# Queries loaded in rows of eight tokens and kept in permuted order, with a new order of the whole program

## The chip, the cores and the metric

The kernel runs on one core of one Trainium2 chip. The metric is the device time of one execution in microseconds, as the median of a few runs. A core has five engines with an instruction queue each: TensorE (PE), VectorE (DVE), ScalarE (ACT), GpSimd (POOL) and SyncE (SP). They wait for each other by semaphores. Loads and stores are DMAs, issued here from the queues of POOL and SP and carried out by 16 DMA engines that work for the core.

## The reference, cut to what matters

q, k and v are float32 of shape (8 batches, 8 heads, 576 tokens, 64). w_q and w_k are (512, 64), w_out is (512, 512), the result is (8, 576, 512).

```
scores = q @ k^T / 8
rel    = pos_q - pos_k
scores = where(0 <= rel < 128, scores - slope[head] * |rel|, -1e9)
x      = softmax(scores) @ v                    # heads side by side: (8, 576, 512)
wq, wk = x @ w_q, x @ w_k
mixed  = (wq @ wk^T / 8) @ x                    # over all 576 tokens, no softmax
out    = relu(mixed) @ w_out
```

Each query sees itself and the 127 tokens before it. The second half mixes all tokens of a batch linearly, so the kernel computes wk^T @ x (64 by 512) once per batch and multiplies wq by that.

## The kernel before, in words

All inputs are cast to float16 by the DMAs that load them, except the first ones of batch 0. Per batch b the operations have names, which stand in the order string (line 35) and in this text:

- **Lq, Lk, Lv, Lt** load q, k, v in blocks of 128 tokens, and the last 64 tokens ("tails") of q and k of two batches together (`add_loads`, line 405). A load of one block moves, for 128 tokens and 8 heads, 1024 pieces of 256 bytes. The tile `nat` holds q and k as loaded, in a ring of four batches; `natt` holds the tails, `vt` and `vtl` hold v.
- **Lf, Lh** load q and k of batch 0 in rows of four tokens (`add_first`, line 388), Lf from SP and uncast.
- **TQ** turns q and k by transposes on TensorE, so that the head dimension lies in the partitions (`add_tq`, line 471, and `add_tq0`, line 447, for batch 0). TQb.0 turns q and k of token blocks 0 and 1, TQb.2 those of blocks 2 and 3, 32 transposes each of 64 partitions by 128 columns. **ETQ** copies the result from PSUM (tile `pair`) to `qkT`. TT and ETT do this for the tails.
- **QK** multiplies 128 keys with the 256 queries that can see them, two heads at a time (`add_unit`, line 521). **EXP** is the exponential on ScalarE, from PSUM into `pt`; **MUL** on VectorE multiplies with `bias`, the exponential of the distances with the mask (`add_mul`). `bias` and `biasl` (for the last group) are made once, from a table of distances that POOL's iota writes (line 312).
- **PV** multiplies with v (`add_pv`, line 566); **R** and **X** on VectorE divide by the sums into `x`. PVb.4 does the tails of two batches.
- **XT, EXT** turn x; **WQ, EWQ, EWD, WKT, EWK, G, EG** make wq, wk and wk^T @ x; **MX, RM** mix and apply the relu; **OUT, EO** multiply with w_out and copy to `osb`; **DO** stores 128 tokens (line 819). Stores of batches 0 to 5 go from POOL, and each of them waits until all loads have been issued (line 876); `osb` has 26 buffers (HELD), so that early results are held until then. Stores of batches 6 and 7 go from SP.

The order of everything is written out by hand in the string ORDER: each word is an operation, the engine it runs on, for TensorE the PSUM banks, and after a + how many filling matmuls (of zeros, into the same bank) stand ahead of it. `Graph.ordered` (line 145) emits them in that order, so each engine's queue is the string's words for that engine. An engine takes its queue strictly in order. Copies out of PSUM may stand on ScalarE or VectorE, as the string says.

The waits are set from the operations' dependencies; TQ waits for its loads, a load into the ring waits for the TQ that read the old contents four batches before.

Of the kernel before, what the change touches and what calls it, by code (L numbers as in the profile page):

```python
# [9 lines left out]
F16 = mybir.dt.float16  # L10
# [30 lines left out]
ETQ0.1.1.1@DVE TT0@PE:1 EXP0.0.1@ACT Lv0.3@POOL QK0.1.1@PE:0 EXP0.2.0@ACT Lk1.0@POOL MUL0.0@DVE
QK0.2.1@PE:3 EXP0.1.1@ACT Lv0.2@POOL ETT0@DVE ETT1@DVE QK0.3.1@PE:2+1 Lq1.1@POOL EXP0.2.1@ACT MUL0.1@DVE
Lq1.0@POOL TQ1.2@PE:0+1 EXP0.3.1@ACT MUL0.2@DVE PV0.0@PE:1 Lk1.1@POOL ETQ1.2@ACT QK0.3.0@PE:3 R0.0@DVE
biasl1@DVE Lv0.4@POOL EXP0.3.0@ACT QK1.3.1@PE:2+1 X0.0@DVE QK1.3.0@PE:0 Lv1.3@POOL EXP1.3.1@ACT
MUL0.3@DVE PV0.1@PE:3 Lv1.2@POOL EXP1.3.0@ACT R0.1@DVE Lw1@POOL PV0.2@PE:2+2/10 X0.1@DVE QK1.2.0@PE:1
R0.2@DVE PV0.3@PE:0 X0.2@DVE EXP1.2.0@ACT Lq2.1@POOL XT0.0@PE:3 R0.3@DVE MUL1.3@DVE QK1.2.1@PE:2
Lq2.0@POOL EXP1.2.1@ACT TQ1.0@PE:1 X0.3@DVE Lv1.1@POOL EXT0.0@ACT ETQ1.0@DVE XT0.1@PE:2 Lk2.0@POOL
EXT0.1@ACT PV0.4@PE:0 Lk2.1@POOL QK1.1.0@PE:1 R0.4@DVE QK1.0.0@PE:3 X0.4@DVE EXP1.1.0@ACT QK1.1.1@PE:2
pads@POOL MUL1.2@DVE WQ0.0@PE:00 Lv1.0@POOL EXP1.1.1@ACT QK1.0.1@PE:1 XT0.2@PE:01 Lk2.3@POOL EXT0.2@DVE
EXP1.0.0@ACT MUL1.1@DVE WQ0.1@PE:01 Lk2.2@POOL PV1.3@PE:2 EXP1.0.1@ACT PV1.2@PE:3 R1.3@DVE Lq2.2@POOL  # L50
X1.3@DVE EWQ0.0@ACT XT1.2@PE:10 EWQ0.1@ACT R1.2@DVE Lq2.3@POOL X1.2@DVE WKT0@PE:11+1 TQ2.0@PE:2 EWK0@DVE
Lwo2@POOL EXT1.2@DVE ETQ2.0@ACT G0@PE:11 MUL1.0@DVE Lwo1@POOL XT1.1@PE:0 EG0@ACT Lwo3@POOL QK2.0.0@PE:3
EXT1.1@ACT PV1.0@PE:2 Lwo0@POOL PV1.1@PE:1 EXP2.0.0@ACT R1.0@DVE Lt2.0@POOL X1.0@DVE QK2.0.1@PE:0
EWD0@ACT R1.1@DVE WQ1.1@PE:30 Lt2.1@POOL EXP2.0.1@ACT X1.1@DVE MX0.0@PE:2 EWQ1.1@DVE Lv2.1@POOL
XT1.0@PE:1 RM0.0@DVE TQ2.2@PE:0 EXT1.0@ACT Lq3.2@POOL MX0.1@PE:3 ETQ2.2@ACT WQ1.0@PE:10 RM0.1@DVE
Lk3.2@POOL EWQ1.0@ACT QK2.1.1@PE:2 EWD1@ACT QK2.2.0@PE:0 Lk3.3@POOL MUL2.0@DVE WKT1@PE:11 EXP2.1.1@ACT
QK2.2.1@PE:3 OUT0.3@PE:10 Lq3.3@POOL EWK1@DVE EXP2.2.1@ACT G1@PE:11 Lq3.0@POOL EO0.3@DVE EXP2.2.0@ACT
QK2.1.0@PE:2 EG1@DVE TT2@PE:3 Lv2.0@POOL OUT0.2@PE:10 ETT3@DVE EXP2.1.0@ACT ETT2@DVE Lk3.0@POOL
QK2.3.0@PE:0 EO0.2@DVE MX1.0@PE:3 EXP2.3.0@ACT MX1.4@PE:2 Lv2.2@POOL OUT0.0@PE:11 RM1.0@DVE Lk3.1@POOL
RM1.4@ACT MX1.1@PE:0 EO0.0@ACT QK2.3.1@PE:2 MUL2.2@DVE OUT0.1@PE:10 Lq3.1@POOL RM1.1@ACT MUL2.1@DVE  # L60
# [105 lines left out]
def kernel(  # L166
# [145 lines left out]
    def mk_iota(o):  # L312
        nc.gpsimd.iota(wint, pattern=[[1, 256]], base=0, channel_multiplier=-1)
# [603 lines left out]
```

## Time and profile before

| | |
|---|---|
| median of 3 runs | 134.95 us (134.85 to 134.96) |
| the profiled execution | 135.62 us, its span 133.6 us |
| around the span | 2.0 us |
| granted TensorE clock, mean | 0.974 |
| DMA packets | 111431, of which 105840 under 512 B |
| moved by DMA | 25.12 MB, mean 188 GB/s |
| HBM read and written | 29.62 MB and 9.44 MB |

The profile gives the busy time of each engine, then groups of instructions by line, with their count, their total and the mean duration of one in ns, and the idle time before them with what ended it. A row of the instructions in order of time has start, time covered, engine, line, tiles and shapes. A stretch of several equal instructions is one row, and its time is that of the whole stretch, in which neighbours overlap. "issue" as a reason means that the profile shows nothing that the engine waited for. A tile name such as nat stands for all its buffers. The DMA share in a table by stage is a mean over the 16 engines of the time of the packets under way, which can be more than one at once.

### The profile page before, as it was taken

How to read it: one execution, taken by the hardware profiler on the slowest of the kernel's cores; microseconds unless marked ns; L12 is line 12 of the kernel's file. 1: busy time of each engine (PE TensorE's matmuls, PEld its weight loads, DVE VectorE, ACT ScalarE, POOL GpSimd, SP SyncE). 2: the span in 40 equal slices, each digit the busy share in tenths (PEclk: the TensorE clock that was granted, in tenths of full speed). 3: DMA queues.
4: the chain of work that ended last, by engine and by line, in shares of the span. 5: the costliest groups of instructions: out<-in, count | busy, mean ns of one | idle time of the engine just before them, and what ended most of it. 6: DMA issues, size and time to landing. Idle time of an engine off the chain costs nothing.

```text
span 133.6 us, 5403 instructions
## 1 busy us (share of the span) xinstructions
PE 120.6 (90%) x2356; PEld 78.1 (58%) x2356; DVE 110.2 (82%) x186; ACT 113.1 (85%) x166; POOL 109.7 (82%) x148
## 2 busy tenths in 40 slices
PE   6884999689889999999999999999999899999950
PEld 2551567556646566757766576667666556775520
DVE  6528888899898999998997999999999899968240
ACT  6778886697999999999999999999999899765630
POOL 7985999999999999999999999999966158871000
PEclk9999658999999999999999999999999999999999
DMA  3999999999999999999999999999999729998973
GB/s 107 259 167 157 157 151 152 140 148 142 183 155 160 153 155 152 154 156 157 159 149 152 156 154 156 158 151 154 155 202 395 302 93 285 355 326 304 355 264 94
DMA packets 111431, 25.12 MB, mean 188 GB/s; under 512 B 105840, under 2 KB 108656, under 8 KB 111408
## 3 DMA queue, kind: packets, MB, share of 16 engines
q0 software_dynamic: 108896, 21.37, 179.4%
q1 hardware_dynamic: 2512, 3.41, 7.4%
q8 instruction: 18, 0.29, 0.9%
q14 instruction: 5, 0.04, 0.1%
HBM read 29.62 MB, written 9.44 MB: 292 GB/s over the span
## 4 chain that ended last, share of the span: by engine, by line
PE 46%; ACT 23%; DMA 11%; POOL 7%; DVE 6%; issue 4%; ACTq 0%; POOLq 0%; DVEq 0%
PE pair L229 40%; ACT pt L551 13%; DMA natt<-in_q_dram 7%; PE pair L232 5%; DMA vt<-in_v_dram 5%; POOL nat L380 4%; ACT qkT L242 3%; DVE x L615 2%; ACT osb L236 2%; DVE pt L561 2%; ACT rm L755 1%; ACT wqd L242 1%; POOL vt L380 1%; DVE inv L612 1%; ACT gs L236 1%
## 5 line engine op out<-in xcount | busy, mean ns | idle before, releaser
L551 ACT ACTIVATE pt<-pair 128x1024 f16<-128x1024 f32 x64 | 63.2, 1039 | 4.0 <-PE pair L229 2.6
L229 PE MATMUL pair<-wout_sb,rm 128*128 128x512 f16 (+1 forms) x132 | 31.9, 373 | 0.2 <-ACT wkn L242 0.2
L380 POOL DMA_DIRECT2D vt<-in_v_dram x32 | 30.2, 1044 | 2.1 <-DMA natt<-in_q_dram 1.6
L561 DVE TENSOR_TENSOR pt<-pt,bias 128x2048 f16<-128x2048 f16 x24 | 29.0, 1216 | 1.4 <-ACT pt L551 1.4
L380 POOL DMA_DIRECT2D nat<-in_q_dram x29 | 27.8, 988 | 0.3 <-issue 0.2
L380 POOL DMA_DIRECT2D nat<-in_k_dram x29 | 27.7, 993 | 0.0
L229 PE MATMUL pair<-qkT 64*128 64x256 f16 (+2 forms) x320 | 23.6, 258 | 0.8 <-ACT qkT L242 0.3
L229 PEld LDWEIGHTS <-pt 128*128 128x128 f16 (+1 forms) x576 | 19.3, 102 | 7.1 <-issue 3.2
L615 DVE TENSOR_TENSOR x<-pair,inv 128x512 f16<-128x512 f32 x32 | 22.1, 690 | 0.9
L229 PE MATMUL pair<-vt,pt 128*128 128x65 f16 (+1 forms) x512 | 22.0, 196 | 0.6 <-DMA vt<-in_v_dram 0.5
L822 POOL DMA_DIRECT2D out_dram<-osb x24 | 13.4, 576 | 8.1 <-DVE osb L238 4.3
L229 PEld LDWEIGHTS <-rm 128*128 128x128 f16 x132 | 11.4, 97 | 11.2 <-issue 1.2
L236 ACT COPY osb<-pair 128x512 f32<-128x512 f32 (+1 forms) x24 | 13.7, 582 | 3.9 <-PE pair L229 3.2
L229 PEld LDWEIGHTS <-qkT 64*128 64x128 f16 x320 | 11.8, 97 | 7.6 <-issue 3.1
L242 ACT COPY qkT<-pair 128x1024 f32<-128x1024 f32 (+1 forms) x13 | 12.7, 980 | 1.3 <-PE pair L232 1.1
L757 DVE TENSOR_SCALAR rm<-pair 128x1024 f16<-128x1024 f32 (+1 forms) x10 | 11.0, 1113 | 1.6 <-PE pair L229 1.5
L238 DVE COPY osb<-pair 128x512 f32<-128x512 f32 x13 | 8.9, 687 | 4.0 <-PE pair L229 3.9
L232 PE MATMUL pair<-identh,nat 64*128 64x64 f16 (+1 forms) x512 | 10.6, 194 | 0.7 <-ACT pt L551 0.3
L229 PE MATMUL pair<-xT,wqk_sb 128*128 128x256 f16 (+1 forms) x64 | 10.1, 286 | 0.9 <-DVE xT L244 0.4
L232 PEld LDWEIGHTS <-nat 64*128 64x128 f16 (+1 forms) x512 | 9.3, 98 | 2.8 <-issue 1.3
L612 DVE RECIPROCAL inv<-pair 128x8 f32<-128x8 f32 x36 | 7.3, 203 | 4.1 <-PE pair L229 3.2
L561 DVE TENSOR_TENSOR pt<-pt,biasl 128x2048 f16<-128x2048 f16 x8 | 9.7, 1207 | 0.4 <-ACT pt L551 0.4
(73 smaller groups left out, 165.1 us busy)
## 6 DMA issues: line engine op xcount, KB each, us to landing
out_dram<-osb POOLq DMA_DIRECT2D x24, 256.0 KB, 5.1
vt<-in_v_dram POOLq DMA_DIRECT2D x32, 128.0 KB, 5.9
nat<-in_q_dram POOLq DMA_DIRECT2D x28, 128.0 KB, 5.5
nat<-in_k_dram POOLq DMA_DIRECT2D x28, 128.0 KB, 5.5
out_dram<-osb SPq DMA_DIRECT2D x7, 256.0 KB, 2.9
out_dram<-osb POOLq DMA_DIRECT2D x6, 128.0 KB, 4.9
nat<-in_q_dram SPq DMA_DIRECT2D x1, 512.0 KB, 3.9
nat<-in_k_dram SPq DMA_DIRECT2D x1, 512.0 KB, 4.9
```

The source lines that it names most:

```text
L229: hold(nc.tensor.matmul(*a, **k))
L232: hold(nc.tensor.transpose(*a))
L236: hold(nc.scalar.copy(out_ap, in_ap))
L238: hold(nc.vector.tensor_copy(out=out_ap, in_=in_ap))
L242: hold(nc.scalar.copy(out_ap.bitcast(FP32), in_ap.bitcast(FP32)))
L380: op = add(kind, b, part, (eng,), deps, lambda o: q.dma_start(out=dst, in_=src), size=size)
L551: nc.scalar.activation(out=pt[:, u, 0:1024], in_=two(s.bank).rearrange("p e c -> p (e c)"), func=AF.Exp, scale=SCALE)
L561: nc.vector.tensor_tensor(out=pt[:, :, 0:1024], in0=pt[:, :, 0:1024], in1=bt, op=ALU.mult)
L612: nc.vector.reciprocal(out=box["inv"], in_=px(64))
L615: nc.vector.tensor_tensor(out=x.rearrange("p (g h d) -> p g h d", g=2, h=4), in0=px(slice(0, 64)), in1=box["inv"].unsqueeze(3).broadcast_t ...
L757: hold(nc.vector.tensor_scalar(out=out_ap, in0=in_ap, scalar1=0.0, scalar2=WSCALE, op0=ALU.max, op1=ALU.mult))
L822: q.dma_start(out=out[b, P * st:P * st + P, c], in_=osb)
```

## The change

**Loads of q, batches 1 to 7.** The four loads of a batch become two. Lqb.0 takes heads 0 to 3, Lqb.1 heads 4 to 7. Each has 64 partitions with 4 heads of 8 successive tokens: 256 pieces of 2 KB of float32, into half of the partitions of `nat`. Partition p of a half holds tokens 8p to 8p + 7. k and v are loaded as before.

**Turning.** TQb.0 now turns all of q of a batch, TQb.1 all of k. q takes 64 transposes of 64 by 64 (head half e, head group u), two of which share the rows and two the columns of TensorE's array; k takes 32 of 64 by 128. The first QK of a batch thus needs all of q and k, where it needed blocks 0 and 1.

**The order of queries.** Turning leaves the queries sorted by token mod 8; ETQ writes them so that each block of 128 tokens has 8 groups of 16, group t holding the tokens with token mod 8 = t. Everything behind the scores carries that order (rows of pt, x, wq, mixed, osb). The table of distances is written in the same order (iota), and `biasl`, whose last quarter belongs to the tails in their plain order, is made by three copies in place of two. For batch 0, whose q is loaded in rows of four tokens, each copy of q becomes four copies of a quarter. The stores put the rows back: a store goes to 8 groups of 16 rows, each row 2 KB.

**The order string** is new as a whole. Operations move between ScalarE and VectorE, and the filling matmuls go from 17 to 31, now with the last of them before XT0.1.

```
-iota@POOL Lf0.0@SP ident@POOL Lf1.0@SP dist@DVE mask@DVE Lh0.1@POOL empty@DVE bias0@ACT Lh1.1@POOL
+iota@POOL Lf1.0@SP ident@POOL Lf0.0@SP dist@DVE empty@DVE pads@POOL ones@DVE Lh1.1@POOL mask@DVE
...
-        nc.gpsimd.iota(wint, pattern=[[1, 256]], base=0, channel_multiplier=-1)
+        nc.gpsimd.iota(wint, pattern=[[128, 2], [1, 8], [8, 16]], base=0, channel_multiplier=-1)
...
-            for c, n in ((0, 192), (192, 64)):
-                cpw(o.eng, dst[:, :, c:c + n], src[:, :, 0:n])
+            cpw(o.eng, dst[:, :, 0:P], src[:, :, 0:P])
+            for c, a in ((P, P), (192, 0)):
+                cp(o.eng, dst[:, :, c:c + 64].rearrange("p x (q t) -> p x q t", t=8),
+                   src[:, :, a:a + P].rearrange("p x (t q) -> p x q t", t=8)[:, :, 0:8])
...
+                    elif n < 2:
+                        loads[b, j, n] = load(
+                            "Lq", b, n, ("c", 256, 2048), old,
+                            nat_s[b % NNAT][j][64 * n:64 * n + 64].rearrange("p n h d -> p (n h d)").rearrange(
+                                "p (h c) -> p h c", h=4),
+                            t[b, 4 * n:4 * n + 4, 0:512, :].rearrange("h (p t) d -> p h (t d)", t=8))
...
+                    for c in range(2):
+                        for r in range(2):
+                            cp(o.eng, dst[:, c].rearrange("p (n r t q) -> p r n t q", n=2, r=2, t=4)[:, r],
+                               src[:, c].rearrange("p t (n q r) -> p r n t q", n=2, r=2)[:, r])
...
+                for c in range(2):
+                    for t in range(8):
+                        for e in range(2):
+                            for u in range(2):
+                                r = slice(64 * u, 64 * u + 64)
+                                tp(bank[64 * e:64 * e + 64, u, c, t], rows[r, 2 * c + e, t], identh[r, r])
...
+                cpw(o.eng, dst.rearrange("p c (n t q) -> p c t n q", n=4, t=8),
+                    bank.rearrange("p u (c t n q) -> p (u c) t n q", c=2, t=8, n=4))
...
-            need = [evt[b, g], evt[b, g + 1]] if g < 3 else [evt[b, 3], ett[b]]
+            need = [evt[b, 0], evt[b, 1]] + ([] if g < 3 else [ett[b]])
...
-                q.dma_start(out=out[b, P * st:P * st + P, c], in_=osb)
+                q.dma_start(out=out[b, P * st:P * st + P, c].rearrange("(p t) c -> t p c", t=8), in_=osb)
```

POOL's queue near the program's start, before (nat10 and nat11 are q and k of batch 1, nat20 and nat21 those of batch 2; the shape is partitions x pieces x elements):

```order
L380 DMA nat10_75<-in_q_dram 128x8x64
L380 DMA vt_85<-in_v_dram 128x8x64 x3
L380 DMA nat11_76<-in_k_dram 128x8x64
L380 DMA vt_85<-in_v_dram 128x8x64
L380 DMA nat10_75<-in_q_dram 128x8x64 x2
L380 DMA nat11_76<-in_k_dram 128x8x64
L380 DMA vtl_86<-in_v_dram 64x16x64
L380 DMA vt_85<-in_v_dram 128x8x64 x2
L380 DMA wqk_sb_71<-in_moe_w_k_dram 128x4x64
L380 DMA nat20_77<-in_q_dram 128x8x64 x2
L380 DMA vt_85<-in_v_dram 128x8x64
L380 DMA nat21_78<-in_k_dram 128x8x64 x2
```

and now, the same stretch:

```order
L381 DMA nat10_75<-in_q_dram 64x4x512
L381 DMA nat11_76<-in_k_dram 128x8x64 x2
L381 DMA vt_85<-in_v_dram 128x8x64 x4
L381 DMA nat21_78<-in_k_dram 128x8x64
L381 DMA vt_85<-in_v_dram 128x8x64
L381 DMA nat20_77<-in_q_dram 64x4x512
L381 DMA vtl_86<-in_v_dram 64x16x64
L381 DMA nat20_77<-in_q_dram 64x4x512
L381 DMA nat21_78<-in_k_dram 128x8x64 x3
L381 DMA wqk_sb_71<-in_moe_w_q_dram 128x4x64
```

The last load of batch 2's q or k stands a few rows behind vtl now (the end of the x3 row); before, four of its eight loads came later than the rows shown.

ScalarE's queue in batches 0 and 1, before (L551 is EXP, L242 and L236 are copies out of PSUM: qkT is ETQ, xT is EXT, wqk is EWQ):

```order
L242 COPY qkT_84<-pair_117 128x2x8x2x32
L551 ACTIVATE pt_90<-pair_120 128x1024
L551 ACTIVATE pt_91<-pair_119 128x1024
L551 ACTIVATE pt_91<-pair_117 128x1024
L551 ACTIVATE pt_88<-pair_118 128x1024
L551 ACTIVATE pt_88<-pair_119 128x1024
L242 COPY xT_103<-pair_120 128x2x4x2x32
L242 COPY xT_103<-pair_119 128x2x4x2x32
L551 ACTIVATE pt_87<-pair_118 128x1024
L551 ACTIVATE pt_87<-pair_119 128x1024
L551 ACTIVATE pt_92<-pair_120 128x1024
L551 ACTIVATE pt_92<-pair_118 128x1024
```

and now, from the copy of batch 1's q on (L580 is EXP, L241 a copy):

```order
L241 COPY qkT_84<-pair_117 128x4x8x4x8
L580 ACTIVATE pt_90<-pair_119 128x1024
L580 ACTIVATE pt_91<-pair_117 128x1024
L580 ACTIVATE pt_92<-pair_118 128x1024
L580 ACTIVATE pt_91<-pair_119 128x1024
L580 ACTIVATE pt_92<-pair_120 128x1024
L580 ACTIVATE pt_88<-pair_119 128x1024
L580 ACTIVATE pt_87<-pair_120 128x1024
L241 COPY xT_103<-pair_117 128x2x4x2x32
L580 ACTIVATE pt_88<-pair_120 128x1024
L580 ACTIVATE pt_87<-pair_118 128x1024
```

Seven exponentials stand in a row where there were five and then two copies of turned x; on TensorE, PV0.4 stood ahead of four of batch 1's score units (QK1.1.0, QK1.0.0, QK1.1.1, QK1.0.1) and stands ahead of one now (QK1.2.0).

SP's queue at the end, before (L822 is a store of 128 tokens, L825 one of 64):

```order
L822 DMA out_dram<-osb_2964 128x512
L822 DMA out_dram<-osb_2982 128x512
L822 DMA out_dram<-osb_2989 128x512
L825 DMA out_dram<-osb_2992 64x512 x2
```

and now:

```order
L851 DMA out_dram<-osb_3204 8x16x256
L851 DMA out_dram<-osb_3212 8x16x512
L854 DMA out_dram<-osb_3220 64x512 x2
L851 DMA out_dram<-osb_3228 8x16x512
L851 DMA out_dram<-osb_3231 8x16x512
```

The two stores of 64 tokens stood last and stand third from the end now; a store's DRAM side has 8 groups of 16 rows in place of 128 rows.

More of the change, by code (lines that the diff above doesn't have):

```diff
@@ L41 @@
[L41 to L60, printed above, removed]
@@ L118 @@
+DO7.4@SP OUT7.0@PE:01 EO6.0@DVE DO6.0@SP EO7.0@ACT DO7.0@SP
 """
@@ L495, in add_tt @@
+        old = [qkd.get((b - 2, g, u)) for g in range(4) for u in range(2)]
+        evt[b, j] = add("ETQ", b, j, EV, [t, *old], ev, frees=[t], size=2)
     def add_tt(pr):
```

201 lines of the change are left out of this document (113 added, 88 removed).

## The prediction

> **What bounds the kernel now.** I read the page first, then the busy time by stage, then the instructions in order of time around the holes, then the chain.
>
> ```profile
> span 133.6 us, 5403 instructions
> PE 120.6 (90%) x2356; PEld 78.1 (58%) x2356; DVE 110.2 (82%) x186; ACT 113.1 (85%) x166; POOL 109.7 (82%) x148
> PE 46%; ACT 23%; DMA 11%; POOL 7%; DVE 6%; issue 4%; ACTq 0%; POOLq 0%; DVEq 0%
> ```
>
> The third line is the chain that ended last: mostly TensorE, then ScalarE, with loads and their issuing on GpSimd (DMA and POOL, 18%) before that. By stage, columns PE, PEld, DVE, ACT, POOL busy, then clock, DMA share and GB/s:
>
> ```profile
> 10.00:20.00 10.00, 7.87 (x119) 4.56 (x119) 8.24 (x13) 8.61 (x10) 8.41 (x10) 0.71 2.41 155
> 20.00:30.00 10.00, 8.28 (x193) 6.19 (x190) 8.62 (x14) 7.44 (x10) 10.00 (x16) 0.95 2.36 147
> 30.00:40.00 10.00, 9.08 (x203) 6.05 (x201) 9.13 (x16) 8.74 (x15) 9.84 (x14) 1.00 2.01 160
> 60.00:70.00 10.00, 9.91 (x219) 6.99 (x219) 9.27 (x18) 9.67 (x15) 10.00 (x13) 1.00 2.42 155
> 90.00:100.00 10.00, 9.74 (x224) 7.01 (x222) 9.61 (x17) 9.90 (x13) 8.95 (x13) 1.00 2.40 167
> ```
>
> Three regimes. From 40 us on TensorE, ScalarE, VectorE and GpSimd are all over 90% busy: nothing there gets faster unless work goes away. From 10 to 40 us ScalarE idles 1.39 + 2.56 + 1.26 = 5.2 us while GpSimd does nothing but issue loads. And at the end TensorE runs alone. So the change, which takes work from GpSimd alone, can only pay in the second regime. The three largest ScalarE holes there:
>
> ```profile
> 22.18 1.02 ACT L551 ACTIVATE pt<-pair 128x1024 f16<-128x1024 f32 x1 [1.09 <-issue]
> 25.71 0.19 PE L229 MATMUL pair<-vt,pt 128*64 128x65 f16 x1 [0.51 <-DMA vt<-in_v_dram]
> 26.75 3.77 ACT L551 ACTIVATE pt<-pair 128x1024 f16<-128x1024 f32 x4 [1.06 <-PE pair L229]
> 31.98 1.01 ACT L242 COPY qkT<-pair 128x1024 f32<-128x1024 f32 x1 [0.87 <-PE pair L232]
> ```
>
> 1.09 + 1.06 + 0.87 = 3.0 us. The second has its cause in the row above it: PV0.4 waits for a v load on TensorE, with the scores of batch 1 queued behind it. The third waits for TQ2.0, the turning of batch 2's q and k.
>
> **The change part by part.** *Loads.* Prices of a POOL load, start to start, from rows with 1024, 512 and 128 pieces:
>
> ```profile
> 1.63 0.90 POOL L380 DMA_DIRECT2D nat<-in_q_dram  x1
> 2.53 0.78 POOL L380 DMA_DIRECT2D nat<-in_k_dram  x1
> 27.33 1.81 POOL L380 DMA_DIRECT2D nat<-in_k_dram  x2
> 29.07 1.82 POOL L380 DMA_DIRECT2D nat<-in_q_dram  x2
> 30.80 2.24 POOL L380 DMA_DIRECT2D wout_sb<-in_moe_w_out_dram  x4
> 32.91 0.96 POOL L380 DMA_DIRECT2D natt<-in_q_dram  x1
> 94.44 2.16 POOL L380 DMA_DIRECT2D vt<-in_v_dram  x2
> ```
>
> 1024 pieces of 256 B: (29.07 - 27.33)/2 = 0.87 us. 128 rows of 2 KB: (32.91 - 30.80)/4 = 0.53. 512 rows of 1 KB: 0.75 to 0.90. A new q load has 256 rows of 2 KB; I take 0.62, nearer the 2 KB rows. 28 x 0.87 - 14 x 0.62 = 24.4 - 8.7 = 15.7 us less on GpSimd (bounds 11.8 at 0.90, 16.9 at 0.53). None of it is on the end's path after 40 us. What it moves: batch 2's last q or k load is issued at 29.07 + 0.87 = 29.9 now. In the new queue nothing but 22 loads and three memsets stands before Lk2.3; added up at these prices from about 2 us, that is 21 us, and an estimated 23.5 with waits for earlier loads. The last load of all, at 95.3 us now, would go near 81. So TQ2.0 and TQ2.1 can run some 6 us sooner. PV0.4 also moves: it stood ahead of four score units of batch 1, in the new order ahead of one, so that its wait no longer blocks ScalarE.
>
> I count the three holes as gone: -3.0. Against it stands a late start. The q copies of batch 0 now go in four pieces each:
>
> ```profile
> L236 ACT CAST wkn<-pair 128x128 f16<-128x128 f32 x1 | 0.3, 266 | 0.0
> 7.44 1.07 ACT L236 CAST qkT<-pair 128x512 f16<-128x512 f32 x2 [1.67 <-PE pair L229]
> 8.51 1.94 ACT L551 ACTIVATE pt<-pair 128x1024 f16<-128x1024 f32 x2
> ```
>
> Four times 0.266 is 1.06, in place of one of some 0.6: the first exponential comes at about 8.95, not 8.51, +0.45. Start: -2.55 (bounds: -4.75 if all 5.2 us go; -0.65 if one hole goes).
>
> *ScalarE's load.* Beyond its place, the order gives work to ScalarE. Counted up to the last exponential it gets 4 output copies, 4 of wkn, 2 tails, 3 of wq, 2 small relus, 1 of xT more; 3 of G, 3 large relus, 1 of qkT fewer; and three added pieces. The main prices:
>
> ```profile
> L236 ACT COPY osb<-pair 128x512 f32<-128x512 f32 x22 | 13.0, 601 | 3.4 <-PE pair L229 2.8 <-DMA out_dram<-osb 0.6
> L755 ACT ACTIVATE rm<-pair 128x1024 f16<-128x1024 f32 x6 | 6.3, 1043 | 0.7 <-PE pair L229 0.7
> L236 ACT CAST gs<-pair 128x256 f16<-128x256 f32 x5 | 1.9, 373 | 0.1
> L242 ACT COPY wkn<-pair 128x160 f32<-128x160 f32 x2 | 0.6, 292 | 0.2
> L242 ACT COPY qkT<-pair 128x256 f32<-128x256 f32 x1 | 0.4, 372 | 0.0
> L236 ACT CAST wqk<-pair 128x320 f16<-128x320 f32 x4 | 1.8, 454 | 0.2 <-PE pair L229 0.2
> ```
>
> 4 x 0.60 + 4 x 0.29 + 2 x 0.37 + 3 x 0.42 (between gs and the 320 row) + 2 x 0.39 + 0.58 - 3 x 0.37 - 3 x 1.04 - 1.03 + 0.47 = +2.1 us by durations. But instructions that follow each other overlap: four exponentials took 3.77 us in the row at 26.75, so each after the first costs 0.91, 0.13 less than its 1.04. With 12 instructions more that takes 1.5 off: +0.6, which I take; the ends are 0.6 and 2.1. VectorE gets about as much less, which helps only where it was late. The added q copy in runs of 16 is priced as before, since it moves the same 128x1024 words.
>
> *TensorE.* Per batch q is turned by 64 transposes of 64 by 64 in place of 32 on 64 by 128. Both kinds are in the trace:
>
> ```profile
> 8.88 0.45 PE L232 MATMUL pair<-identh,nat 64*64 64x64 f16 x32
> 23.25 0.64 PE L232 MATMUL pair<-identh,nat 64*128 64x64 f16 x32
> L232 PE MATMUL pair<-identh,nat 64*64 64x64 f16 x64 | 0.9, 195 | 0.2 <-DMA nat<-in_k_dram 0.2
> L232 PEld LDWEIGHTS <-nat 64*64 64x64 f16 x64 | 0.7, 108 | 0.6 <-DMA nat<-in_k_dram 0.3 <-issue 0.2
> ```
>
> One takes 195 ns, but 32 take 0.45 us, so they follow at (0.45 - 0.195)/31 = 8 ns; the half-array ones at (0.64 - 0.19)/31 = 14.5. 64 x 8 - 32 x 14.5 = 0.05 to 0.07 us per batch, seven times: +0.5. At 14.5 each it would be 7 x 0.46 = +3.3, the upper bound. [...] The 14 extra fill matmuls stand before 25 us, where TensorE waits anyway.
>
> *The tail.* Behind the last scores TensorE has one OUT more (OUT5.2), without WQ6.0 and XT7.2:
>
> ```profile
> 110.44 1.89 PE L229 MATMUL pair<-wout_sb,rm 128*128 128x512 f16 x8
> 109.99 0.61 PE L229 MATMUL pair<-xT,wqk_sb 128*128 128x256 f16 x4
> 109.97 1.95 ACT L551 ACTIVATE pt<-pair 128x1024 f16<-128x1024 f32 x2
> 128.96 0.58 ACT L236 COPY osb<-pair 128x512 f32<-128x512 f32 x1 [1.60 <-PE pair L229]
> 122.48 6.72 SPq L822 DMA_DIRECT2D out_dram<-osb  x9
> 129.56 1.16 SPq L825 DMA_DIRECT2D out_dram<-osb  x2
> out_dram<-osb SPq DMA_DIRECT2D x7, 256.0 KB, 2.9
> out_dram<-osb SPq DMA_DIRECT2D x4, 128.0 KB, 2.6
> ```
>
> An OUT paces at about 0.9 us ((1.89 - 0.3)/2, and its start), a WQ at 0.45: +0.3 with XT7.2. The last store was two of 128 KB, issued in 1.16; now one of 256 KB, issued in 0.36 (as the nine in 6.72, less waits): -0.8, and its landing 2.9 for 2.6: +0.3. Together -0.5. That the last rows are strewn 16 KB apart in DRAM I price at nothing here; they are still whole 2 KB rows.
>
> Sum: -2.55 + 0.6 + 0.5 + 0.3 - 0.5 = -1.65. The profiled execution took 135.62 (span 133.6), 0.67 above the median of 134.95; it would become 133.97, and the median 133.3.
>
> **The rivals.** *Slower: ScalarE is the limit and the holes move.* The mechanism: in the middle the chain passes to ScalarE for 23% of the span, and each microsecond given to it there is paid. The price is the full 2.1, the late first exponential 0.45, one hole recovered -1.1, tail +0.3 - 0.5: +1.25, 136.2. It decides once less than 2.5 us of the 5.2 idle on ScalarE before 40 us go. For it: ScalarE is 97 to 99% busy later. Against it: VectorE is relieved, and no hole of the start lay in ScalarE itself.
>
> *The stores go at half rate.* A store's DRAM side is now 8 groups of 16 rows, where it was 128 rows. If only half of the DMA engines serve such a store, the transfer part of its landing doubles: 2.9 - 2.6 = 0.3 per 128 KB, so 0.6 more for the last, and nine stores issued in 6.72 us would need about 8 x 1.2 = 9.6 us of transfer, a queue of up to 2.9 us; I count a third of it, since the last four stores come 0.9 apart: +0.9, and +1.5 in all, 134.8. Nothing in this trace shows it: every load and store there has an outermost count of 64 or 128. [...]
>
> *The loads do not come sooner.* If the bytes set the pace and not the pieces, a q load of 512 KB read takes as long as two old ones (2 x 0.87) and the issue saving is taken back by transfers. Then PV0.4 alone gains by its place: of the three holes half go, +1.5 on the sum, 134.8. For it: the DMA engines show a share over 2 in every stage; against it, weight loads of 2 KB rows go at 0.53, and the share fell to 2.01 behind them.
>
> **How the numbers follow.** A measurement of this kernel can tell about 0.2% (0.27 us). Forecast 133.3: 0.45. Slower rival 136.2: 0.25. Half-rate stores 134.8: 0.18. Loads no sooner 134.8: 0.12. The middle two lie at -0.1%, so each is split: of their 0.30, 0.11 faster, 0.11 same, 0.08 slower. Faster: 0.44 + 0.11 = 0.55, same 0.01 + 0.11 = 0.12, slower 0.25 + 0.08 = 0.33. Range: down to all 5.2 us of the start recovered, 133.3 - 2.2 = 131.1; up to the slower rival with 0.3 for drains between transposes, 136.5.
>
> **What would show it.** Right: POOL q loads of some 0.62 us start to start; the last load issued near 81 us; ScalarE busy over 9 of 10 us from 20 to 30 us; blocks of 64 small transposes in 0.7 us. The slower rival shows as the last exponential ending later than 109.97 + 1.95 = 111.9 us, where it ends now. Half-rate stores show as SP stores of 256 KB landing 3.5 us or more after issue. Wrong altogether: idle ScalarE after 40 us, behind TensorE, which would mean that the new order has holes of its own.

## The result, and the profile after

The changed kernel takes 155.3 us (154.95 and 155.61), the kernel before beside it 134.9 (134.2 to 134.96): a ratio of 1.149 (1.142 to 1.155), 20 us slower where 1.65 us faster was forecast. (Times in this document are medians of the executions within 1.5% of the fastest of their kernel, one for `e1_plain` and two for the changed kernel; the profiled executions of `e1_plain`, `h2_double_plain`, `f3_before_twice` and `h3_half_paced` lie outside, so stops and waits are read from them but no total times.) The profiled execution took 155.61 us, its span 153.8.

The page of the changed kernel: span, busy time by engine, two queues and the chain that ended last.

```profile
span 153.8 us, 5894 instructions
PE 125.3 (81%) x2594; PEld 79.8 (52%) x2594; DVE 110.1 (72%) x189; ACT 116.0 (75%) x177; POOL 96.0 (62%) x134
...
q0 software_dynamic: 85120, 21.38, 137.7%
q1 hardware_dynamic: 2440, 3.41, 7.0%
q8 instruction: 20, 0.33, 0.8%
...
PE 57%; ACT 12%; issue 11%; DVE 10%; POOL 0%; POOLq 0%; ACTq 0%; DVEq 0%
```

GpSimd's busy time fell by 13.7 us, near the 15.7 forecast, and it has gone from the chain (7% before). In its place stands "issue" with 11% (4% before): time in which an engine waited for nothing that the profile shows. By stage, as in the prediction's table:

```profile
10.00:20.00 10.00, 8.01 (x229) 4.66 (x223) 6.25 (x13) 9.28 (x11) 9.12 (x11) 1.00 2.13 168
20.00:30.00 10.00, 8.68 (x247) 5.93 (x238) 9.49 (x16) 7.85 (x10) 7.96 (x10) 1.00 2.09 168
30.00:40.00 10.00, 7.61 (x140) 5.50 (x139) 6.38 (x13) 7.14 (x11) 9.19 (x13) 0.83 1.80 178
60.00:70.00 10.00, 9.90 (x222) 6.95 (x219) 9.10 (x18) 9.65 (x16) 9.03 (x12) 1.00 2.18 165
90.00:100.00 10.00, 8.07 (x166) 5.85 (x160) 6.37 (x13) 6.50 (x11) 7.18 (x13) 0.83 1.45 231
```

In some stages TensorE, VectorE and ScalarE are each idle for 1.9 to 3.6 us (30 to 40, 90 to 100). The granted clock is 0.83 in these two: it is 0.5 for 3.4 us from 33.4 and from 94.9 us, about 1 us behind the end of the two longest stops below, and matmuls are slower there as well (one of 128x320 took 473 ns from 33.4 to 36.8 us, 297 from 36.9 to 50). TensorE's waits for loads come to 0.4 us in all. Its part in the list of waits (total us, times, longest) and what it did there:

```profile
PE pair L231 <- issue: 8.9, 6, 2.4
...
PEld L231 <- issue: 13.4, 19, 2.5
```

```profile
28.86 0.70 PE L231 MATMUL pair<-identh,nat 64*64 64x64 f16 x64 [0.34 <-ACT xT L241]
...
29.83 0.22 PE L231 MATMUL pair<-identh,nat 64*128 64x64 f16 x2
32.45 0.59 PE L231 MATMUL pair<-identh,nat 64*128 64x64 f16 x29 [2.39 <-issue]
```

The block of 64 small transposes takes 0.70 us, as priced. Then TensorE stops for 2.4 us in the middle of k's transposes, whose loads have landed. Before, the same view has 4.7 us in 15 waits, the longest 0.7, and the page fewer pieces on queue q8:

```profile
PEld L232 <- issue: 4.7, 15, 0.7
...
q8 instruction: 18, 0.29, 0.9%
```

Counted from 0 in the records of the trace, weight loads, matmuls and a few waits together (5188 and 13), the stops of over 1 us in 64-partition transposes come at TensorE's instructions 705, 1217, 2241, 3009, 3777 and 4289: all of them 193 + 256 k. Queue q8 brings instructions, 20 pieces of 16 KB here and 18 before, against 5201 and 4721 TensorE instructions: one piece for about 256. So I call a **gap** the time between the starts of instructions 192 + 256 k and 193 + 256 k where it is over 0.4 us, and a fetch's **delay** the time from the start of instruction 193 + 256 k to the start of the next piece on q8 (mean over blocks begun from 15 to 95 us). Before: no gap, delay 2.07 us. After: gaps of 10.0 us in all, delay 3.25 us.

The end moved as well. Last output copy and SP's stores, of the changed kernel:

```profile
139.62 0.59 ACT L235 COPY osb<-pair 128x512 f32<-128x512 f32 x1 [1.14 <-PE pair L228]
132.49 10.12 SPq L851 DMA_DIRECT2D out_dram<-osb  x7
142.71 3.13 SPq L854 DMA_DIRECT2D out_dram<-osb  x2
145.93 1.36 SPq L851 DMA_DIRECT2D out_dram<-osb  x2
out_dram<-osb SPq DMA_DIRECT2D x4, 128.0 KB, 6.7
```

From the end of the last copy to the end of the span it takes 153.8 - 140.2 = 13.6 us, where it took 133.6 - 129.5 = 4.1. (Of the four stores of 128 KB one has a recorded landing.) And behind 140 us, with nothing but stores left, the DMA engines are half busy (last two columns: share and GB/s):

```profile
135.00:140.00 5.00, 4.58 (x32) 2.27 (x24) 1.81 (x3) 2.98 (x7) 0.00 (x0) 1.00 0.68 188
140.00:145.00 5.00, 0.00 (x0) 0.00 (x0) 0.00 (x0) 0.20 (x1) 0.00 (x0) 0.76 0.52 174
145.00:150.00 5.00, 0.00 (x0) 0.00 (x0) 0.00 (x0) 0.00 (x0) 0.00 (x0) 0.50 0.57 155
```

So two things are to be explained: some 10 us of TensorE stops, and some 10 us of stores.

### The profile page after: what moved, and what is told of

It is laid out like the page before. It is cut to its first block, busy times and chain, and to the rows that moved or that the text cites. A ratio compares the mean times of both kernels' runs of the same rounds, so it can differ in the third digit from the quotient of the medians.

```text
span 153.8 us, 5894 instructions
## 1 busy us (share of the span) xinstructions
PE 125.3 (81%) x2594; PEld 79.8 (52%) x2594; DVE 110.1 (72%) x189; ACT 116.0 (75%) x177; POOL 96.0 (62%) x134
## 3 DMA queue, kind: packets, MB, share of 16 engines
q0 software_dynamic: 85120, 21.38, 137.7%
## 4 chain that ended last, share of the span: by engine, by line
PE 57%; ACT 12%; issue 11%; DVE 10%; POOL 0%; POOLq 0%; ACTq 0%; DVEq 0%
PE pair L228 49%; PE pair L231 8%; ACT pt L580 6%; DVE pt L590 4%; ACT bias L345 2%; ACT osb L235 2%; DVE x L644 2%; ACT qkT L235 1%; DVE qkT L243 1%; ACT biasl L235 1%; DVE inv L641 1%; DVE vtl L330 1%; DVE xtl L644 0%; DVE nat L316 0%; ACT xT L241 0%
## 5 line engine op out<-in xcount | busy, mean ns | idle before, releaser
L580 ACT ACTIVATE pt<-pair 128x1024 f16<-128x1024 f32 x64 | 63.3, 1033 | 6.8 <-PE pair L228 6.4
L381 POOL DMA_DIRECT2D vt<-in_v_dram x32 | 28.5, 896 | 2.8 <-DMA nat<-in_q_dram 1.4
L381 POOL DMA_DIRECT2D nat<-in_k_dram x29 | 25.8, 898 | 5.6 <-DMA vt<-in_v_dram 4.0
L851 POOL DMA_DIRECT2D out_dram<-osb x24 | 14.4, 603 | 23.7 <-ACT rmt L784 17.3
L235 ACT COPY osb<-pair 128x512 f32<-128x512 f32 (+1 forms) x29 | 16.7, 582 | 4.7 <-PE pair L228 4.6
L231 PE MATMUL pair<-identh,nat 64*64 64x64 f16 (+1 forms) x736 | 11.1, 193 | 7.3 <-issue 7.0
L231 PEld LDWEIGHTS <-nat 64*64 64x64 f16 (+1 forms) x736 | 9.2, 104 | 9.8 <-issue 8.7
L241 ACT COPY qkT<-pair 128x1024 f32<-128x1024 f32 (+1 forms) x14 | 12.4, 886 | 1.6 <-PE pair L231 1.6
L786 DVE TENSOR_SCALAR rm<-pair 128x1024 f16<-128x1024 f32 (+1 forms) x11 | 12.3, 1124 | 1.0 <-PE pair L228 0.7
L228 PE MATMUL pair<-xT,wqk_sb 128*128 128x256 f16 (+1 forms) x64 | 11.5, 314 | 0.1
L228 PE MATMUL pair<-fill 128*128 128x512 f16 x31 | 9.5, 437 | 1.4 <-DVE fill L361 1.2
L381 POOL DMA_DIRECT2D nat<-in_q_dram x15 | 9.9, 662 | 1.1 <-DMA nat<-in_q_dram 0.5
L590 DVE TENSOR_TENSOR pt<-pt,biasl 128x2048 f16<-128x2048 f16 x8 | 9.7, 1217 | 0.7 <-ACT pt L580 0.7
```

The costliest lines, as they stand in the source:

```text
L228: hold(nc.tensor.matmul(*a, **k))
L231: hold(nc.tensor.transpose(*a))
L235: hold(nc.scalar.copy(out_ap, in_ap))
L241: hold(nc.scalar.copy(out_ap.bitcast(FP32), in_ap.bitcast(FP32)))
L381: op = add(kind, b, part, (eng,), deps, lambda o: q.dma_start(out=dst, in_=src), size=size)
L580: nc.scalar.activation(out=pt[:, u, 0:1024], in_=two(s.bank).rearrange("p e c -> p (e c)"), func=AF.Exp, scale=SCALE)
```

## The experiments

Times with the 95% interval of the ratio to the kernel before. Gaps and delays are those of the one profiled execution of each.

| run | us | ratio | TensorE instructions | delay | gaps, us |
|---|---|---|---|---|---|
| before | 134.9 | 1 | 4721 | 2.07 | 0 |
| after | 155.3 | 1.142 to 1.155 | 5201 | 3.25 | 10.0 |
| `e1_plain` | 144.3 | one run | 5201 | 3.48 | 12.4 |
| `e2_sixteen` | 145.1 | 1.064 to 1.088 | 5201 | 3.28 | 9.5 |
| `e3_before_groups` | 147.7 | 1.083 to 1.107 | 4721 | 1.97 | 0.9 |
| `e4_before_rows` | 137.0 | 1.003 to 1.026 | 4721 | 2.79 | 4.4 |
| `f3_before_twice` | 137.0 | 1.007 to 1.022 | 5169 | 2.18 | 2.3 |
| `h1_half_plain` | 136.7 | 1.008 to 1.021 | 4753 | 3.07 | 1.9 |
| `h2_double_plain` | 144.7 | 1.066 to 1.084 | 5201 | 3.30 | 9.3 |
| `g1_mix` | 149.6 | 1.100 to 1.121 | 5201 | 2.87 | 6.5 |
| `e5_paced` | 137.7 | 1.013 to 1.026 | 4721 | 1.68 | 1.2 |
| `d1_after_paced` | 140.8 | 1.038 to 1.052 | 5201 | 1.88 | 2.9 |
| `e6_rows_first` | 135.7 | two runs | 4721 | 1.86 | 2.0 |
| `e7_both_rows` | 138.3 | 1.021 to 1.041 | 4721 | 2.73 | 3.2 |
| `h3_half_paced` | 139.4 | 1.032 to 1.041 | 4753 | 1.96 | 0 |
| `d2_paced_all` | 142.2 | 1.053 to 1.060 | 5201 | 1.70 | 0 |

### The stores: `e1_plain`, `e2_sixteen`, `e3_before_groups`

The first two alter only the stores of the changed kernel (`e1_plain` above, `e2_sixteen` below), the third puts its store into the kernel before.

```
-q.dma_start(out=out[b, P * st:P * st + P, c].rearrange("(p t) c -> t p c", t=8), in_=osb)
+q.dma_start(out=out[b, P * st:P * st + P, c], in_=osb)
...
+q.dma_start(out=out[b, P * st:P * st + P, c].rearrange("(p t) c -> t p c", t=16), in_=osb)
```

> The changed kernel, but each store of 128 tokens goes to 128 rows of DRAM in the order in which they lie in osb, so the output rows of a block stay in the order of the queries (token mod 8). All else is as changed. Half-rate theory (only 8 of the 16 DMA engines serve a store with 8 groups): the 9.5 us at the end go, last compute to end of span falls from 13.6 to about 4 us, the run takes 146 to 147 us, SP's 128 KB stores land within 3 us of their issue; last compute stays near 140 us, since the TensorE stalls stay. Rival, the stores queue only because they were held back on GpSimd by the order of the stores: the end stays about 13 us after the last compute.

> The changed kernel, but a store has 16 groups of 8 rows on its DRAM side where it had 8 groups of 16; the rows of a block are strewn over DRAM as in the changed kernel, but land in other places than they should. Theory that the number of groups sets how many DMA engines serve a store: as with plain rows, 146 to 147 us and some 4 us from last compute to the end. Rival, rows strewn 16 KB apart in DRAM cost the time (pages, address jumps): as the changed kernel, some 155.6 us and 13 us.

> The kernel before, with one edit: each store of 128 tokens goes to 8 groups of 16 rows, as in the changed kernel, so the rows land in other places than they should. Half-rate theory: last compute to the end of the span grows from 4.1 us to 11 to 14 us and the time to 142 to 145 us; last compute stays near 129.5. Rival, the end of the changed kernel is late because of its order and not because of its groups: within 1 us of 135.

Measured: 144.3, 145.1 and 147.7 us; the theory's ranges were missed by 1 to 3 us, below for the first two and above for the third. From the end of the last copy to the end of the span it takes 3.8 us with plain rows (as in `h1_half_plain` below) and 4.6 with 16 groups, against 13.6 with 8, though with 16 groups the rows of a group lie twice as far apart in DRAM (32 KB in place of 16). So strewn rows are not the main cause, the number of groups is. In the kernel before, 8 groups alone cost 12.8 us. Its SP stores, its last copy, and its end by stage:

```profile
122.10 15.07 SPq L822 DMA_DIRECT2D out_dram<-osb  x9
137.27 2.90 SPq L825 DMA_DIRECT2D out_dram<-osb  x2
128.58 0.59 ACT L236 COPY osb<-pair 128x512 f32<-128x512 f32 x1 [1.60 <-PE pair L229]
130.00:135.00 5.00, 0.00 (x0) 0.00 (x0) 0.00 (x0) 0.00 (x0) 0.00 (x0) 0.75 0.62 179
135.00:140.00 5.00, 0.00 (x0) 0.00 (x0) 0.00 (x0) 0.00 (x0) 0.00 (x0) 0.50 0.53 190
```

The nine stores take 15.07 us to issue, where they took 6.72, though SP waited for their data no longer than before (2.5 us, 3.3 before): it is held by something that no view names. The last copy stays (129.2, before 129.5), and 16.6 us of storing follow it in place of 4.1. The same stage of `e2_sixteen`:

```profile
135.00:140.00 5.00, 3.05 (x15) 1.18 (x12) 1.38 (x2) 1.95 (x5) 0.00 (x0) 1.00 0.93 289
```

A share of 0.93 at 289 GB/s against 0.53 at 190. The half-rate theory has 8 of the 16 DMA engines serve a store with 8 groups. The trace does not tell the engines apart, so that itself is not shown, but these shares, near a half with 8 groups and near the whole with 16, agree with it. The rivals written down for the three runs fall. So does one that the changed kernel's page suggests: GpSimd stands still for 17.3 us ahead of one store there, and the DMA share from 110 to 120 us is 0.07. In `e2_sixteen` the same wait is 16.4 us long, and its stores still end 4.6 us after the last copy.

### The stops: `e4_before_rows`, `h1_half_plain`, `h2_double_plain`, `f3_before_twice`

If TensorE stops because its next 256 instructions have not come, two things make it: instructions used up faster, and fetches that come later. These four runs separate the two. `e4_before_rows` gives the kernel before the large q loads (each turning of a batch then waits for both of them):

```
+elif n < 2:
+    loads[b, j, n] = load("Lq", b, n, ("c", 256, 2048), old,
+        nat_s[b % NNAT][j][64 * n:64 * n + 64].rearrange("p n h d -> p (n h d)").rearrange(
+            "p (h c) -> p h c", h=4),
+        t[b, 4 * n:4 * n + 4, 0:512, :].rearrange("h (p t) d -> p h (t d)", t=8))
```

`h1_half_plain` and `h2_double_plain` (with its inner loop) take the changed kernel with plain stores, and other transposes of q; `f3_before_twice` does each q transpose of the kernel before twice:

```
-for e in range(2):
-    for u in range(2):
-        r = slice(64 * u, 64 * u + 64)
-        tp(bank[64 * e:64 * e + 64, u, c, t], rows[r, 2 * c + e, t], identh[r, r])
+for u in range(2):
+    r = slice(64 * u, 64 * u + 64)
+    for _ in range(2):
+        tp(bank[:, u, c, t], flat[r, 8 * c + t], identh[r, r])
...
+for _ in range(2 - j):
     flip(halves(o.bank, 8, len(ns))[:, h, NHP * j + c, i, :], src.rearrange("p a b -> p (a b)"), h)
```

> The kernel before, with q of batches 1 to 7 loaded by two DMAs of 256 pieces of 2 KB in place of four of 1024 pieces of 256 B; everything else, the order too, as before (the values of q land in other places than the transposes take them from, so the scores are wrong). My forecast's theory of the loads: GpSimd is some 15 us less busy, the loads come sooner, and one or two of the three holes of ScalarE before 40 us shrink: 132 to 134.5 us. Rival, the larger loads delay TensorE's instruction fetches and so make the stalls by themselves: 138 us or more, with gaps at every 256th instruction. Third, loads no sooner: 134.9 within 0.5.

> The changed kernel with stores to plain rows and with the q of batches 1 to 7 turned by 32 transposes of 64 by 128 a batch (the arrangement of q in qkT is then not the one that the scores need) in place of 64 of 64 by 64: 448 TensorE instructions less. Measured against e2_sixteen (145.1 us, with 9.5 us of gaps at TensorE instructions 193 + 256 k). Fetch theory (TensorE stalls where the next 256 instructions have not been fetched, because the 64-transposes use them up faster than the fetches come): the gaps fall to about what e4_before_rows has, 3 to 5 us, and the time to 137 to 140 us. Rival, small transposes cost by changing the array's tiling: the gaps go wholly, 135.5 us or less. Rival, the gaps come from the loads and the order alone: they stay, 144 to 145 us.

> As h1_half_plain, but each of the 32 transposes of q is done twice: the number of TensorE instructions is that of the changed kernel again (5201), with no transpose of 64 by 64 for q. Fetch theory: gaps at instructions 193 + 256 k with a sum of 8 to 11 us, 143.5 to 147 us. Rival, the tiling by 64 by 64 makes the gaps: as h1_half_plain, within 1.5 us of it.

> The kernel before, with each transpose of q of batches 1 to 7 done twice: 448 TensorE instructions more, loads, order and stores as before. Fetch theory: gaps of over 0.4 us appear at instructions 193 + 256 k, fewer than with the 2 KB loads, whose fetches start later (mean 2.1 us after the block before, 2.8 to 3.3 there): a sum of 2 to 6 us, and the time up by as much and by 7 x 0.5 us of transposing, 138 to 144 us. Rival, gaps come with the 2 KB loads alone: no gap over 0.4 us, 135 to 139 us.

In `e4_before_rows` TensorE runs the program of the kernel before, instruction by instruction, and stops nevertheless: 1.58, 0.45, 1.21, 0.71 and 0.46 us, each at 193 + 256 k. With the loads alone changed the delay went from 2.07 to 2.79 us, and the kernel is 2.1 us slower, not 0.4 to 2.9 us faster: my theory of the loads missed, its rival (138 or more) was a little high.

448 transposing instructions more cost 2.1 us with the old loads (`f3_before_twice`, gaps 2.3 us, the time a little below its forecast) but 8.4 us with the new (`e2_sixteen` less `h1_half_plain`, gaps 7.6 us more) or 8.0 (`h2_double_plain` less `h1_half_plain`). These pairs differ in the order of the program too; the next section has a pair that does not. And the tiling is not what makes the stops: `h2_double_plain`, without a 64-by-64 transpose of q in batches 1 to 7, is as slow as `e2_sixteen`, and stops at the same place for as long as the changed kernel did. (Its 64 larger transposes take 1.11 us in place of 0.70, some 3 us in seven batches, so the equal times by themselves leave room for a small cost of the tiling; there is one, shown with the term for TensorE below.)

```profile
28.78 1.11 PE L231 MATMUL pair<-identh,nat 64*128 64x64 f16 x64 [0.34 <-ACT xT L241]
...
32.64 0.59 PE L231 MATMUL pair<-identh,nat 64*128 64x64 f16 x29 [2.58 <-issue]
```

In `h1_half_plain`, with gaps and time a little below what the fetch theory gave, the stops of TensorE's transposes have shrunk to 1.1 us at most:

```profile
PE pair L231 <- issue: 1.5, 2, 1.0
PEld L231 <- issue: 6.1, 15, 1.1
```

What a stop needs can be read from the records. In the changed kernel the block of 256 instructions begun at 26.52 us is used up at 29.86; the next piece starts on q8 at 30.12 and takes 0.96 us, and TensorE goes on at 32.45. In all runs, where a fetch was late, TensorE went on 2.2 to 3.2 us after the fetch's start, of which its transfer is about 1.0. So 256 instructions must last for the delay and about 2.4 us. Before, 2.07 + 2.4 = 4.5 us, and its fastest block lasted 4.5 us: no gap, but no margin either. After, 3.25 + 2.4 = 5.65 us, and blocks lasted from 3.3 us on.

### The order put right elsewhere: `g1_mix`

```
+rhs = w[r][h, src:src + n]
+if at < 512:
+    rhs = rhs.rearrange("p (k t q) -> p k q t", t=8, q=16)
-mm(pm[:, r, n * d:n * d + n], g[h, P * d:P * d + P], w[r][h, src:src + n], start=True, stop=True)
+mm(pm[:, r, n * d:n * d + n], g[h, P * d:P * d + P], rhs, start=True, stop=True)
```

> The changed kernel, with the order of the tokens put right in the mixing in place of the stores: the mixing matmuls read the 128 queries of a block in the order of the tokens (16 runs of 8 with a step of 32 bytes between neighbours), so mixed, osb and the stores have plain rows. Everything is computed. If such a reading costs nothing: as e2_sixteen, 144.5 to 146 us. If TensorE reads strided columns at a quarter or less of its pace: a mixing matmul of 256 columns takes 0.6 us and more where it takes some 0.25, 64 of them, up to 25 us more. Half-rate theory of the stores: some 4 us from the last compute to the end.

Measured: 149.6 us. The store's price is gone (SP's 256 KB stores land 2.0 us after issue), but a part of it is paid on TensorE: a mixing matmul of 256 columns takes 628 ns, where it takes 271 in `h1_half_plain`.

```profile
L228 PE MATMUL pair<-wqd,gs 64*128 64x256 f16 x28 | 14.8, 628 | 0.0
L228 PE MATMUL pair<-wqk,gs 64*128 64x256 f16 x28 | 14.8, 628 | 0.0
```

The second case held for the matmul's time, which is 2.3 times as long (a quarter of the pace is not shown), but the kernel lost only 4.5 us against `e2_sixteen`. The gaps fell to 6.5 us, which fits blocks that last longer and so leave the fetches more time; that this is the reason is not shown.

### Why the fetches come late: `e5_paced`, `d1_after_paced`, `e6_rows_first`, `e7_both_rows`

`e5_paced` and `d1_after_paced` slow GpSimd down behind each large load; `e6_rows_first` has large q loads in batches 1 and 2 alone, `e7_both_rows` for k too.

```
+q.dma_start(out=dst, in_=src)
+if kind == "Lq" and b > 1:
+    for _ in range(4):
+        nc.gpsimd.memset(junk, 0.0)
...
+if j or b > 2:
...
+for n in range(2):
+    for j, t in enumerate((q, k)):
```

> As e4_before_rows (the kernel before with q in 2 KB rows), but behind each q load of batches 2 to 7 GpSimd writes four times 256 zeros a partition into a tile that nothing reads, about 1.2 us, the issue time that the larger loads save. Fetches of TensorE instructions start 2.07 us after the block before in the kernel before and 2.79 us in e4_before_rows (means from 15 to 95 us). Theory A, the fetch waits behind larger packets (1024 B written in 100 ns where 128 B took 33 ns): the delay stays 2.6 to 3 us and the time at 136.5 to 138 us. Theory B, the fetch waits because GpSimd fills the queue faster than it drains: the delay falls to 2.0 to 2.3 us, the gaps of over 0.4 us after 20 us go, 133 to 135.3 us.

> As e2_sixteen (the changed kernel with 16 groups of 8 rows in its stores, 145.1 us, fetch delay 3.28 us, gaps 9.5 us), with the same 1.2 us of zeros on GpSimd behind each q load of batches 2 to 7. Theory A (packet size): 144.5 to 146 us, delay over 3 us. Theory B (a queue filled faster than it drains): the delay falls to some 2.2 us, the gaps to 3 to 6 us, 139 to 142.5 us.

> The kernel before, with q in 2 KB rows for batches 1 and 2 alone (whose values then lie in other places than the transposes take them from); batches 3 to 7 are loaded as before. If the gain of the start that I forecast exists and the later gaps of e4_before_rows (1.21 + 0.71 + 0.46 us behind 64 us) are what ate it: 133 to 134.6 us. If the start gains nothing from earlier loads: 135 to 136.5 us, with gaps before 30 us alone.

> The kernel before, with q and k of batches 1 to 7 both in 2 KB rows (values in other places than the transposes take them from): the suspected cost of e4_before_rows doubled. If large loads delay the fetches: mean delay 3.3 us or more, gaps of 6 to 10 us, 138 to 142 us. If the delay has nothing to do with the size of the pieces: 2.1 to 2.8 us, 135 to 137 us. The loads are then issued so soon that the first stages may gain up to 2 us.

With the packets as large as ever, pacing brought the delay from 2.79 to 1.68 us and from 3.28 to 1.88, below that of the kernel before, and the gaps from 9.5 to 2.9 us: theory A falls, and the pace of the issuing is the cause, as theory B has it. That loads take longer to land is seen in the v loads, which are the same in all kernels: they land 5.9 us after their issue before, 6.9 in `e2_sixteen` and 5.0 in `d1_after_paced` (one line of each page):

```profile
vt<-in_v_dram POOLq DMA_DIRECT2D x32, 128.0 KB, 5.9
vt<-in_v_dram POOLq DMA_DIRECT2D x32, 128.0 KB, 6.9
vt<-in_v_dram POOLq DMA_DIRECT2D x32, 128.0 KB, 5.0
```

Counted in the traces from 15 to 95 us, 5.3 loads on average are issued and not yet landed before, 6.3 and 6.4 in `e2_sixteen` and `e4_before_rows`, 4.1 in `d1_after_paced` and `e5_paced`. GpSimd shows it too: in the changed kernel it waits for the landing of earlier loads before it issues the next, 4.0 us in the largest line of such waits; the two largest before have 1.6 and 0.6 us:

```profile
POOL nat L381 <- DMA vt<-in_v_dram: 4.0, 3, 1.7
```

Pacing also lowers the rate, from 168 to 151 GB/s over the same stretch in the changed kernel (154 before), so whether the number of waiting loads or the rate holds up the fetch is not told apart. `e7_both_rows` came out between its cases: twice as many large loads made no longer delay than `e4_before_rows` (2.73), with 6.4 loads under way again, but the time was 138.3 and not 135 to 137.

The time followed in `d1_after_paced` (145.1 to 140.8 us) but not in `e5_paced`, 137.7 where theory B said 133 to 135.3. The gaps of `e5_paced` behind 20 us are gone, and waits for loads stand in their place:

```profile
PE pair L230 <- DMA nat<-in_k_dram: 1.9, 3, 1.1
PE pair L230 <- DMA nat<-in_q_dram: 1.5, 1, 1.5
```

`e6_rows_first` keeps its late stages as before and is 0.9 us slower than the kernel before (134.8 beside it; two runs): the large loads of the start show no gain in that order. Its gap at 12 us is 1.46 us, and from the 13th exponential on (26.6 us, before 26.7) the two kernels run alike.

### All costs out at once: `h3_half_paced`, `d2_paced_all`

`h3_half_paced` is `h1_half_plain` with the same pacing; in `d2_paced_all` the condition is `kind == "Lq"` alone, in `d1_after_paced`'s kernel.

> As h1_half_plain (the changed kernel with plain stores and 32 transposes a batch for q, 136.7 us), with 1.2 us of zeros on GpSimd behind each q load of batches 2 to 7. All three suspected costs are then out: the stores' groups, the extra transposes, the filled queue. If the rest of my forecast holds (earlier loads at the start bring some 2.5 us, the order costs ScalarE and the tail about 0.9), the time is 133 to 134.6 us. If the new order or the pace of the loads costs what the earlier loads bring: 134.7 to 136 us. If the gaps of h1_half_plain (1.16 + 0.72 us behind 50 us) were of another cause, they stay and the time stays at 136.2 to 137.2.

> As d1_after_paced (140.8 us, gaps of 0.54 and 1.37 us at 13 and 19 us), with the zeros behind the q loads of batch 1 too. If the early gaps come from the filled queue: they fall under 0.5 us together, 139 to 140.2 us. If the first loads, which come one after the other from an empty queue, make them anyway: 140.5 to 142 us.

Both have no gap left, and both are slower than without (more) pacing: 139.4 against 136.7, 142.2 against 140.8. That missed every case that I had written down. TensorE waits for loads now, 7.6 us in all in `d2_paced_all` where it was 2.8 in `d1_after_paced`. The largest lines, first of `d2_paced_all`, then of `h3_half_paced`:

```profile
PE pair L228 <- DMA vt<-in_v_dram: 2.9, 5, 1.1
PE pair L231 <- DMA nat<-in_k_dram: 2.6, 4, 1.0
...
PE pair L228 <- DMA vt<-in_v_dram: 3.6, 4, 1.9
PE pair L231 <- DMA nat<-in_k_dram: 1.9, 3, 1.2
PE pair L231 <- DMA nat<-in_q_dram: 1.2, 1, 1.2
```

The last load is issued at 98.4 us in `h3_half_paced`, at 88.5 in `h1_half_plain`. So the pace of the loads is a bound on both sides: loads that come fast delay TensorE's instructions (a delay of 3.07 us in `h1_half_plain`, 1.96 in `h3_half_paced`), and paced ones its data. No version beat the kernel before.

The four runs with the new order and quick stores also answer what the stops need, since nothing but the transposes of q and the pace changes in them (16 groups or plain rows for the stores aside). With free loads the 448 instructions more cost 8.4 us (136.7 to 145.1), with paced loads 1.4 (`h3_half_paced` to `d1_after_paced`, 139.4 to 140.8). It takes both, instructions used up quickly and fetches that come late.

## Why the prediction was wrong, point by point

**The account.** `h1_half_plain`, without the stores' groups and the extra transposes, is 1.8 us slower than before (136.7 - 134.9); the extra transposes, together with loads issued as fast as they go, add 8.4 (`e2_sixteen` less `h1_half_plain`); the groups add 10.2 (after less `e2_sixteen`). 134.9 + 1.8 + 8.4 + 10.2 = 155.3.

**Start, -2.55.** Right in sign for the new order, and given back. In `h1_half_plain` the 13th exponential starts at 24.9 us, before at 26.7: 1.8 us gained, though the first one came at 10.1 and not at 8.95 (+1.6 where I had +0.45): in the new order VectorE clears tiles before it finishes the table of distances, at 4.3 us where it was 2.4, and ScalarE's eight exponentials of `bias` and its copies start that much later (4.33 and 2.46 us). A part of the gain may be the clock, which the prediction left out: it is 1.00 from 10 to 20 us in the changed kernel, where the prediction's table has 0.71; whether the added filling matmuls did that is not shown. By the last exponential nothing is left (110.8 and 110.9): the gaps of `h1_half_plain`, 1.9 us, lie between. In the changed kernel the gain is 0.9 us at the 13th, and the last one starts at 120.4.

**ScalarE, +0.6.** Not decisive: with the gaps out of the way the last exponential comes when it came before. The test that I gave, its end later than 111.9 us, would have pointed to the wrong rival; ScalarE was idle for 2.9 to 3.5 us in the two stages where most time was lost. "Idle ScalarE after 40 us, behind TensorE", which I had named as the sign of being wrong altogether, is what the trace shows.

**TensorE, +0.5: the step that failed.** "One takes 195 ns, but 32 take 0.45 us, so they follow at 8 ns" was right, as the 0.70 us row shows. But the term counted only the time of the transposes and not what brings the instructions. 64 transposes are 128 instructions in 0.7 us, half of what one fetch brings. Measured: 8.4 us in place of 0.5, and past my bound of 3.3, of which 7.6 are gaps. The 0.3 us for drains between transposes, at the upper end of the range, is a term that no run shows; what the traces show in its place is a small cost at a change of tiling. The turning of batch 6's q behind the same eight matmuls, in the changed kernel and in `h1_half_plain`:

```profile
82.34 0.39 PE L228 MATMUL pair<-qkT 64*128 64x192 f16 x8
82.66 0.71 PE L231 MATMUL pair<-identh,nat 64*64 64x64 f16 x64
...
77.04 0.39 PE L228 MATMUL pair<-qkT 64*128 64x192 f16 x8
77.27 0.63 PE L231 MATMUL pair<-identh,nat 64*128 64x64 f16 x32
```

From the first row of a pair to the second it is 0.32 us with the change of tiling and 0.23 without. Six of the fourteen entries and exits show some 0.1 us more; at most of the others the neighbour's tiling differs in both kernels, and nothing is added. That is 0.6 us in all by my estimate.

**Loads, -15.7 us on GpSimd.** The price was right (0.66 us mean, 13.7 us less busy), the use was not. I expected the last load near 81 us; it went at 88.5, and GpSimd's waits for the landing of loads grew from 2.1 to 7.5 us up to 95 us, which is a good part of the difference. (That GpSimd is over 90% busy from 40 us on held to 90 us; the next stage has 8.95 of 10.) The rival "the loads do not come sooner" came near this, but not to its side effect: with the large loads alone the fetches came later (a delay of 2.79 us in place of 2.07), and `e4_before_rows` lost 2.1 us.

**Stores, a rival at +1.5 with a chance of 0.18.** The sum itself had them at nothing. What the rival supposed, half of the DMA engines for such a store, agrees with the share of 0.53 in `e3_before_groups` and 0.93 with 16 groups, though no trace tells the engines apart; its size was wrong by a factor of seven (10.2 us; 12.8 in `e3_before_groups`). I took the transfer part from the difference of two landings, 0.3 us per 128 KB, which would be 437 GB/s; the stage of `e2_sixteen` in which the DMA engines carry nothing but stores shows 289. And "I count a third of it" relied on the last four stores coming 0.9 us apart; they did not. SP takes 14.8 us from its first store to the end of its last (132.49 to 147.29; 8.2 before), and GpSimd's, still under way beside them until 140.1 us, have slowed down too (256 KB land 7.1 us after issue, 5.1 before). 2.36 MB of SP stores at the 165 GB/s of the end take 14 us.

**The tail, +0.3 - 0.5.** From the last exponential's start to the end of the last copy: 18.65 us before, 19.8 in `h1_half_plain`, so +1.1; behind that 3.8 us in place of 4.1, so -0.2.

**What stays open.** Why a fetch that took 1.0 us to land lets TensorE go on only 2.2 to 3.2 us after its start, and where in the queues the delay of 2 to 3.5 us arises, the traces do not show. The gap near 12 us differs between executions of the same instructions and loads (0.3 us before, 0.9 in `e3_before_groups`, whose program differs only in the stores), so single gaps of 1 us there prove little. Behind 21 us the runs agree: each with a mean delay of 2.7 us or more has gaps of 1.4 us or more in all, each with 2.2 us or less has at most 1.0. How much of the lost time is the low clock behind the long stops was not measured apart.

## What to carry to other kernels

An engine's instructions are loads too: where a kernel issues hundreds of short matmuls in a few microseconds, compare the time in which it uses up 256 of them (from 3.3 us on here) with the time that a fetch needs under the load of that stage (4.5 us before, 5.65 after), and look for "issue" waits at equal counts of instructions. A change that frees the engine which issues loads may only fill the DMA queue, and instruction fetches then come later, as they did here (2.79 us in place of 2.07 in `e4_before_rows`). Check in how many groups a store's rows go out: 8 in place of plain rows cost 12.8 us in `e3_before_groups`. Price a lower rate by bytes over the rate of a stage that does nothing else (289 GB/s here), not by landing times (which gave 437).

## What had not been expected of the hardware

- TensorE stops at its instructions 193 + 256 k where the fetch on queue q8 comes late: up to 2.6 us at a time and 10.0 us in all in the changed kernel, with 18 to 20 fetches of 16 KB in programs of 4721 to 5201 TensorE instructions. Behind the two longest stops the granted clock was 0.5 for 3.4 us.
- In these runs a fetch's delay goes with the pace of the loads and not with the size of their packets: 1.7 to 2.2 us on average with small or paced loads, 2.7 to 3.5 with large loads issued as fast as they go.
- A change between transposes of 64 by 64 and neighbours tiled 64 by 128 cost some 0.1 us (0.32 us from the start of one block to that of the next, 0.23 without it), at six of fourteen places.
- A matmul whose 256 moving columns are read with a step of 32 bytes took 628 ns in place of 271.
- 2 KB rows strewn 32 KB apart in DRAM are stored nearly as fast as contiguous ones, as long as there are 16 groups (2.5 us to land 128 KB, 2.1 with plain rows; the one recorded landing with 8 groups, 16 KB apart, is 6.7).
